# Sums of key weights moved behind row tile 5, and the steps of TensorE in a new order, in a two-branch linear-attention kernel

## The chip, the cores and the metric

The kernel runs on one core of a Trainium2 chip. The metric is the time of one execution on the device, in microseconds; the time before is the median of three runs. One further execution was taken with the hardware profiler, and all views of the profile are of that one. PE is TensorE's matmul, PEld its weight load, DVE is VectorE, ACT is ScalarE, POOL is GpSimd, SP is the engine that issues most DMAs. "L767" is line 767 of the kernel before.

## The reference

Two linear-attention blocks A and B share the input x (2048 x 640, bf16), each with its own weights; 32 heads of 20 columns. A sigmoid gate mixes them.

```python
def _A_ref(x, wqkv, wo):
    qkv = (x @ wqkv).reshape(B, S, 3, H, Dh).transpose(2, 0, 3, 1, 4)
    q, k, v = qkv[0], qkv[1], qkv[2]
    phi = lambda t: jnp.where(t > 0, t + 1, jnp.exp(t)) + 1e-6
    pq, pk = phi(q), phi(k)
    kv = jnp.einsum("bhsd,bhse->bhde", pk, v)
    z = jnp.einsum("bhsd->bhd", pk)
    num = jnp.einsum("bhqd,bhde->bhqe", pq, kv)
    den = jnp.einsum("bhqd,bhd->bhq", pq, z)[..., None] + 1e-6
    o = num / den
    return o.transpose(0, 2, 1, 3).reshape(B, S, D) @ wo
...
x = A_x
g = _sigmoid((x * gate_w).sum(-1, keepdims=True))
a = _A_ref(x, A_wqkv, A_wo)
b = _B_ref(x, B_wqkv, B_wo)
return g * a + (1 - g) * b
```

`_B_ref` is the same function with B's weights.

## The kernel before

Rows of x are worked in 16 tiles of 128. The program is made of operations (`Op`), each for one engine, with the buffers it reads and writes. A list scheduler inside the kernel (`Sched.run`) places them by estimated costs: on VectorE and ScalarE it takes the operation that can start soonest, ties by `prio`; on TensorE it keeps the order in which they were made. So TensorE's order is written out by hand, and the queues of VectorE, ScalarE, SP and GpSimd follow from it. Each queue then runs in order on the chip, with semaphore waits where an operation needs another engine's result. PSUM has 8 banks; a step that takes a bank waits until its last reader is done.

The stages, in TensorE's order:

- K, row tiles 0 to 9, in the order of the loop over `t` (`k_both`, L651 and L652): the keys of A, then of B, five pairs of matmuls each, into two banks. `k_post` makes phi of them: ScalarE's exponential (L699), VectorE's minimum and addition (L702), and then either ScalarE's relu (L711, L726) and a VectorE addition (L717 for both branches at once, L729 for one), or VectorE's L738, which reads the banks itself. `s_pair` (L887) makes differences of the results, which the next stage needs.
- The string `MAIN` orders all that follows. A token names a step:
  - `K14A`: the keys of row tile 14, branch A. `K6.n`: step n of `ks_unit` (L815), which makes the keys of row tiles 12 and 13 in both branches with 7 products in place of 8 (Strassen's scheme, in Winograd's form). It needs sums of the key weights of A and B (`kw_sums`, L767, four VectorE operations) and differences of x (`kx_sums`, L787). Its results are put together on VectorE (`kcm`).
  - `Gg.n`: unit g (0 to 4) of the product of phi(k) transposed with x, in steps 1 to 9 (L1164). VectorE's L1197 (`c11`, `c12`, `c22`) and ScalarE's L1192 and L1271 read the banks; results are moved by transposing DMAs on SP into GSA and GSB.
  - `Qg.n` (L1043): the queries of unit g, first half of the rows; `R0.n` the same for unit 0 of the second half, `R1A` and the like (L1132) the other units of the second half, ten matmuls into two banks, whose readers are ScalarE's L1143 and L1149 or VectorE.
  - `kvA`, `kvB` (L1312): key-value products, from GSA and GSB. `wA0` ... `wB1` (L1344): times the output weights. `dA0` ... `dB1` (L1418): denominators. `T1` stands for four VectorE sums of the resulting weights, `Sb` for VectorE's differences (L1519) of the queries of row block b, `X2` for sums of x, `LA` for a load.
  - `Oi.n` (L1554): the output of 256 rows, pair i (0 to 7), step n of 7. Steps 3 and 4 end with the stores of 128 rows each. ScalarE's L1593, L1570, L1598, L1619 and VectorE's L1577 read the banks.

The sums of key weights use the weights of both branches alone. They are made in the loop over row tiles, where the call stands:

```python
    for t in range(2, KT):
        k_both(t, "AB" if t in RELUB else "A")
        if t % 2:
            s_pair(t // 2)
        if t == 4:
            kw_sums()
    t_all(0, 8)
    kx_sums()
```

Though the call comes behind tile 4, nothing but their inputs holds the four operations back, and the scheduler put them as soon as VectorE had a place for them: among the operations of tiles 0 to 2.

Of the kernel before, what the change touches and what calls it, by code (L numbers as in the profile page):

```python
# [47 lines left out]
KT = 10  # L48
KU = 6
KJ = 7  # L50
KRS = ("10A", "10B", "11A", "11B", "12A", "13B", "14A", "14B", "15A", "15B", "8A", "9A", "9B",)
MAIN = """K14A K6.1 K10A K6.2 K6.5 K6.6 K14B K6.3 K10B K6.7 K11A K11B K6.4 K15A K15B G2.1 G1.1 G2.8 G0.1 G3.1
G1.8 G0.2 G0.8 G0.9 G1.2 G2.2 G2.9 G3.2 G0.6 G0.5 G1.9 G0.7 G3.8 G1.6 G0.3 G2.6 G1.5 G1.7 G0.4 G2.5
G1.3 Q1.1 G2.7 G1.4 Q1.2 Q1.5 Q1.6 G3.9 G3.6 G2.3 Q1.7 Q1.3 Q0.1 Q1.4 Q4.5 Q4.1 Q0.2 Q0.6 Q0.5 G2.4
Q4.6 Q4.2 Q0.7 kvA X2 Q0.3 G4.1 Q4.3 G4.2 G3.5 Q0.4 G4.8 Q4.7 G3.7 Q2.5 G3.3 Q2.1 G3.4 Q3.1 Q2.6
Q2.3 G4.5 Q2.7 G4.6 Q4.4 Q2.2 G4.7 Q3.6 Q3.5 Q3.2 Q3.7 Q2.4 G4.9 G4.3 Q3.4 G4.4 Q3.3 wA0 dA0 R1A
wA1 LA dB0 S1 S0 kvB R4A wB0 R2B R4B R1B wB1 T1 R3B R0.1 R3A R2A R0.6 R0.5 O1.1
R0.2 R0.7 O1.5 R0.3 O3.1 O0.1 O1.2 O3.2 R0.4 O0.2 O3.5 O1.6 O2.1 O1.3 O3.6 O0.6 O2.2 O2.5 O3.7 dA1
dB1 S2 S3 O2.6 O2.3 O1.7 O2.7 O3.3 O0.5 O2.4 O3.4 O0.7 O4.1 O5.1 O6.1 O1.4 O5.2 O4.2 O0.4 O6.2
O5.5 O4.5 O4.6 O7.5 O5.6 O6.6 O6.5 O5.3 O5.7 O6.7 O7.1 O4.7 O5.4 O4.3 O6.3 O7.6 O0.3 O4.4 O7.7 O6.4  # L60
O7.2 O7.3 O7.4"""
RS = (0,)
PB = {}
PQH = (0,)
# [45 lines left out]
class Sched:  # L110
# [9 lines left out]
    def op(self, eng, fn, cost, ins=(), outs=(), after=(), prio=None, name="", dma=None):  # L120
        if eng == "ACT" and dma is None:
            after = list(after) + self.consts
        o = Op(eng, fn, cost, list(ins), list(outs), after, (self.base or len(self.ops)) if prio is None else prio, name, dma)
        self.ops.append(o)
        return o
# [184 lines left out]
def body(nc, A_x, A_wqkv, A_wo, B_x, B_wqkv, B_wo, gate_w, out, log=None):  # L310
# [150 lines left out]
    def dve2(n):  # L461
        return 150 + 0.53 * n
# [178 lines left out]
    pk_last = []  # L641
# [104 lines left out]
    def k_both(t, relu):  # L746
        units = []
        for X in XS:
            ps = Buf("k", "ps", 2, cover=(512, 128))
            for c in range(NC):  # L750
                k_step(X, t, c, ps)
            units.append((X, ps, X in relu))
        k_post(t, units)
# [3 lines left out]
    def kw_sums():  # L757
        a1, a2, b1, b2 = [WK[X][:, c : c + 2, 0 : D + 1] for X in XS for c in (0, 2)]

        def kw(k):  # L760
            return KW[k][:, :, 0 : D + 1]

        for k, in0, in1, how, need in ((1, b1, a1, ALU.subtract, ()), (2, kw(1), b2, ALU.add, (1,)), (3, b1, b2, ALU.add, ()), (4, a2, kw(2), ALU.subtract, (2,))):
            bkw[k] = Buf("kw")
            op(
                "DVE",
                lambda e, k=k, in0=in0, in1=in1, how=how: e.tensor_tensor(out=kw(k), in0=in0, in1=in1, op=how),  # L767
                dve2(1282),
                ins=[bwk[X, c] for X in XS for c in range(4)] + [bgc, bwz] + [bkw[j] for j in need],
                outs=[bkw[k]],  # L770
                name="kw",
            )

# [26 lines left out]
    def ks_unit(j):  # L800
# [22 lines left out]
        def comb(ps, src, into_src):  # L823
            return op(
                "DVE",
                lambda e: e.tensor_tensor(out=kqg(src), in0=psx(ps), in1=kqg(src), op=ALU.add)
                if into_src
                else e.tensor_tensor(out=psw(ps, D + 1), in0=psw(ps, D + 1), in1=KQ[src.slot][:, 0 : D + 1], op=ALU.add),
                dve1(D + 1),
                ins=[ps, src],  # L830
                outs=[src if into_src else ps],
                name="kcm",
            )
# [3 lines left out]
        def step(n):  # L837
# [11 lines left out]
            elif n == 3:  # L849
                mm(pz, D + 1, False, [(WK["B"][:, 2 + c, :], KX[4][:, c, :]) for c in range(2)] + [(WK["B"][:, 4, :], KX[5])], [bkx[4], bkx[5], bgc] + [bwk["B", c] for c in range(2, 5)], [d[5]])  # L850
                comb(pz, s2, False)
                k_post(t1, [("A", py, "%dA" % t1 in KRS), ("B", pz, "%dB" % t1 in KRS)])
            elif n == 7:
                mm(px, D + 1, False, [(KW[3][:, c, :], KX[3][:, c, :]) for c in range(2)], [bkw[3], bkx[3]], [d[2]])
                d[7] = comb(px, s5, True)
            elif n == 4:
                mm(px, D, False, [(KW[4][:, c, :], xt(2 + c, 1)) for c in range(2)] + [(WK["A"][:, 4, :], xt(4, 1))], bx + [bkw[4], bwk["A", 4]], [d[7]])
                for X, ps in (("B", s5), ("A", px)):
                    k_post(t2, [(X, ps, "%d%s" % (t2, X) in KRS)])

# [5 lines left out]
    def s_pair(j):  # L866
        if j % 2 == 0:
            return
        r = range(j - 1, j + 1)
        pk = [bpk[X, t] for X in XS for t in range(2 * j - 2, 2 * j + 2)]  # L870
        for u0, u1 in ((0, 1), (1, NPU)) if j == 7 else ((0, NPU),):

            def pv(h, k):
                return PKv[:, 2 * u0 + h : 2 * u1 : 2, k, j - 1 : j + 1, :]

            def sv(k):
                return SSv[:, u0:u1, k, j - 1 : j + 1, :]

            def sub(out, a, b, ins, d, name):
                bb = Buf(name)  # L880
                for x in r:
                    for u in range(u0, u1):
                        d[u, x] = bb
                s_op.append(
                    op(
                        "DVE",
                        lambda e: e.tensor_tensor(out=out, in0=a, in1=b, op=ALU.subtract),  # L887
                        dve2(2 * (u1 - u0) * 128),
                        ins=ins,
                        outs=[bb],  # L890
                        name=name,
                    )
                )

            k = (u0, j)
            sub(sv(0), pv(1, 0), pv(1, 1), pk, bs1, "s1")
            sub(sv(1), pv(0, 0), sv(0), pk + [bs1[k]], bs2, "s2")
            sub(sv(2), pv(0, 1), sv(1), pk + [bs2[k]], bs4, "s4")
            sub(pv(1, 0), pv(1, 0), pv(0, 0), pk + [bs1[k]], bs3, "s3")
# [48 lines left out]
    for t in range(2, KT):  # L948
        k_both(t, "AB" if t in RELUB else "A")
        if t % 2:  # L950
            s_pair(t // 2)
        if t == 4:
            kw_sums()
    t_all(0, 8)
    kx_sums()
# [203 lines left out]
    def prod(g, name, ps, reg, mov, w, first, ins, after=(), js=(0, 8)):  # L1159
        for j0, j1 in ([(j, j + 1) for j in range(*js)] if g == 0 else [js]):  # L1160

            def fn(e, j0=j0, j1=j1):
                for j in range(j0, j1):
                    r = e.matmul(PS[:, ps.slot, 0:w], reg[:, j, :], mov(j, w), start=(first and j == 0), stop=(j == 7), skip_group_check=not first)  # L1164
                return r

            i = []
            for j in range(j0, j1):
                i += [b for b in ins(j) if b not in i]
            last[name] = op("PE", fn, (j1 - j0) * mm_cost(w), ins=i, outs=[ps], after=after, name="%s_%d" % (name, g))  # L1170
# [3 lines left out]
    def g_unit(g):  # L1174
# [10 lines left out]
        def xv(h, right):  # L1185
            return lambda j, w: (xr if right else xl)(h, j, j + 1, w)[:, 0, :]
# [58 lines left out]
        def step(n):  # L1245
            if n in (1, 8):
                prod(g, "P1", px, ra1, xv(0, False), W, True, lambda j: xn(j, 0) + [bpk[one[0], 2 * j]], js=(0, KJ) if n == 1 else (KJ, 8))
            if n in (2, 9):
                prod(g, "P2", py, ra2, xv(1, False), HC, True, lambda j: xn(j, 1) + [bpk[one[0], 2 * j + 1]], js=(0, KJ) if n == 2 else (KJ, 8))
            if n == 8:  # L1250
# [377 lines left out]
    qsteps = []  # L1628
    kleft = len([t for t in MAIN.split() if t[0] == "K"])
    ks, kps, ktiles, kdone = ks_unit(KU), {}, set(), {j for j in (1, 3, 5) if 2 * j + 1 < KT}  # L1630
    for tok in MAIN.split():
        sch.base = None if tok[0] == "K" else 10**5
        if tok[0] == "K":
# [4 lines left out]
            else:  # L1638
                X, t = tok[-1], int(tok[1:-1])
# [3 lines left out]
                if X == "B":  # L1643
                    k_post(t, [(Y, kps[Y, t], "%d%s" % (t, Y) in KRS) for Y in XS])
                    ktiles.add(t)
# [60 lines left out]
def bass_gated_mix__linear_attn_block__linear_attn_block__prompt_kernel(nc, *args):  # L1706
    body(nc, *args)
# [28 lines left out]
```

## Time and profile before

| | |
|---|---|
| time, median of 3 runs | 175.81 us (175.81 to 176.22) |
| time of the profiled execution | 175.72 us |
| its span in the trace | 174.3 us |
| granted TensorE clock | 1.00 |
| instructions | 3365 |

Where the span goes, by the costliest groups of TensorE and the group that the change moves (line, engine, operation, tiles, shape, count, busy us, mean ns, idle before):

```profile
L651 PE MATMUL ps<-WKW,XT 128*128 128x512 bf16 x140 | 39.4, 382 | 0.2
...
L1164 PE MATMUL ps<-TX,PKS 128*128 128x321 bf16 (+1 forms) x160 | 24.1, 300 | 0.0
L1164 PE MATMUL ps<-XN,PKS 128*128 128x321 bf16 (+1 forms) x120 | 18.3, 300 | 0.0
```

A matmul's busy time covers its whole way through the array, and the next one starts well before it ends: a pair of L651 and L652 comes every 0.27 us, though the two have 0.60 us of busy time. So gaps of TensorE are read from the starts, not from the busy time. Idle time of the other engines costs nothing as long as TensorE goes on.

### The profile page before, as it was taken

The page shows a single profiled execution, that of the slowest core. Times are in us where ns is not written, and L with a number is a line of the kernel's source. Part 1 is how long each engine was busy: PE and PEld are TensorE (multiplying, and loading weights), DVE is VectorE, ACT ScalarE, POOL GpSimd, SP SyncE. Part 2 cuts the span into 40 slices and gives each one's busy share as a digit, 9 for nine tenths or more (in the row PEclk, how much of TensorE's full clock was granted, in tenths as well). Part 3 has the DMA queues.
Part 4 walks back from the last instruction along what each step waited for, and adds up shares of the span by engine and source line. Part 5 has one row for each costly group of instructions (what it writes and reads, how often), then busy time and mean ns, then how long its engine had stood idle before and what let it go on. Part 6 is the DMA issues. An engine that isn't in the chain of part 4 may idle for free.

```text
span 174.3 us, 3365 instructions
## 1 busy us (share of the span) xinstructions
PE 171.6 (98%) x1331; PEld 107.7 (62%) x1331; DVE 140.1 (80%) x246; ACT 115.0 (66%) x221; POOL 4.9 (3%) x17
## 2 busy tenths in 40 slices
PE   9999999999999999999999999999999999999995
PEld 5455555555577776655766655655556667776773
DVE  2298996999999937678975798799999985989441
ACT  5378889998952323558594888848899874366133
POOL 2000000000000080000000000000000000000000
PEclk9999999999999999999999999999999999999999
DMA  6989999990000025310732703277670011451144
GB/s 196 286 152 202 172 367 365 358 171 8 4 0 0 0 41 98 75 38 0 156 79 56 211 0 75 53 196 199 224 184 26 0 41 30 94 186 41 38 148 153
DMA packets 33035, 20.59 MB, mean 118 GB/s; under 512 B 18260, under 2 KB 32892, under 8 KB 33020
## 3 DMA queue, kind: packets, MB, share of 16 engines
q1 hardware_dynamic: 32062, 19.76, 43.4%
q10 hardware_dynamic: 958, 0.63, 1.2%
q8 instruction: 10, 0.16, 0.4%
q14 instruction: 5, 0.04, 0.1%
HBM read 10.88 MB, written 4.26 MB: 87 GB/s over the span
## 4 chain that ended last, share of the span: by engine, by line
PE 96%; DMA 2%; SPq 0%; ACT 0%; issue 0%
PE ps L1164 22%; PE ps L1554 22%; PE ps L651 17%; PE ps L1043 13%; PE ps L1132 10%; PE ps L652 4%; PE ps L815 3%; DMA WKW<-in_A_wqkv_dram 2%; PE ps L1418 1%; PE ps L1344 1%; PE ps L1312 1%; SPq L444 0%; ACT PKS L1619 0%; PE ps L628 0%
## 5 line engine op out<-in xcount | busy, mean ns | idle before, releaser
L651 PE MATMUL ps<-WKW,XT 128*128 128x512 bf16 x140 | 39.4, 382 | 0.2
L652 PE MATMUL ps<-WKW,XT 128*128 128x128 bf16 (+1 forms) x140 | 30.9, 220 | 0.0
L699 ACT ACTIVATE EKT<-ps 128x640 bf16<-128x640 f32 x31 | 21.5, 709 | 5.3 <-PE ps L652 4.8
L651 PEld LDWEIGHTS ps<-WKW,XT 128*128 128x128 bf16 x140 | 13.8, 99 | 17.2 <-DMA WKW<-in_A_wqkv_dram 0.5
L1164 PE MATMUL ps<-TX,PKS 128*128 128x321 bf16 (+1 forms) x160 | 24.1, 300 | 0.0
L1164 PEld LDWEIGHTS ps<-TX,PKS 128*128 128x128 bf16 x160 | 15.6, 98 | 7.4
L1164 PE MATMUL ps<-XN,PKS 128*128 128x321 bf16 (+1 forms) x120 | 18.3, 300 | 0.0
L1164 PEld LDWEIGHTS ps<-XN,PKS 128*128 128x128 bf16 x120 | 11.7, 98 | 5.4
L1192 ACT ACTIVATE EKT<-ps 128x321 f32<-128x321 f32 (+1 forms) x15 | 6.5, 438 | 12.7 <-PE ps L1164 9.0
L652 PEld LDWEIGHTS ps<-WKW,XT 128*128 128x128 bf16 x140 | 13.8, 98 | 0.0
L887 DVE TENSOR_TENSOR PKS<-PKS 128x1280 bf16<-128x1280 bf16 (+2 forms) x20 | 13.1, 684 | 0.1
L1073 ACT ACTIVATE EQ<-ps 128x512 bf16<-128x512 f32 x18 | 10.6, 600 | 3.8 <-DVE ps L1057 2.4
L711 ACT ACTIVATE PKS<-ps 128x640 bf16<-128x640 f32 x16 | 11.3, 708 | 0.0
L1143 ACT ACTIVATE EQ<-ps 128x1024 bf16<-128x1024 f32 x8 | 8.2, 1029 | 4.4 <-PE ps L1132 3.5
L702 DVE TENSOR_SCALAR EKT<-EKT 128x1280 bf16<-128x1280 bf16 (+1 forms) x19 | 8.2, 437 | 3.6 <-ACT EKT L699 3.5
L1043 PE MATMUL ps<-XT,WQA 128*128 128x512 bf16 x36 | 10.4, 379 | 0.0
L1197 DVE TENSOR_TENSOR WKW<-ps,EKT 128x320 bf16<-128x320 f32 x15 | 7.3, 485 | 2.8 <-PE ps L1164 2.6
L1132 PE MATMUL ps<-XT,WQA 128*128 128x512 bf16 x40 | 9.2, 381 | 0.0
L1132 PE MATMUL ps<-XT,WQB 128*128 128x512 bf16 x40 | 9.0, 381 | 0.0
L1619 ACT ACTIVATE PKS<-ps 128x320 bf16<-128x320 f32 x8 | 3.5, 437 | 8.1 <-PE ps L1554 8.1
L738 DVE SCALAR_TENSOR_TENSOR PKS<-ps,EKT 128x640 bf16<-128x640 f32 x10 | 8.1, 818 | 0.0
L1577 DVE TENSOR_TENSOR PKS<-ps,EKT 128x320 bf16<-128x320 f32 x9 | 4.4, 492 | 4.1 <-PE ps L1554 3.8
(179 smaller groups left out, 324.6 us busy)
## 6 DMA issues: line engine op xcount, KB each, us to landing
out_dram<-PKS SPq DMA_DIRECT2D x15, 160.0 KB, 1.8
XN<-in_A_x_dram SPq DMA_DIRECT2D x1, 2240.0 KB, 9.3
WKW<-in_A_wqkv_dram SPq DMA_DIRECT2D x5, 160.0 KB, 3.9
WKW<-in_B_wqkv_dram SPq DMA_DIRECT2D x5, 160.0 KB, 4.3
WQA<-in_A_wqkv_dram SPq DMA_DIRECT2D x1, 800.0 KB, 10.9
WQB<-in_B_wqkv_dram SPq DMA_DIRECT2D x1, 800.0 KB, 12.2
WVA<-in_A_wqkv_dram SPq DMA_DIRECT2D x1, 800.0 KB, 12.0
PKS<-in_B_wqkv_dram SPq DMA_DIRECT2D x1, 800.0 KB, 4.9
```

The source lines that it names most:

```text
L651: e.matmul(a[:, 0:512], l, WK[X][:, c, 0:512], start=(c == 0), stop=(c == NC - 1))
L652: return e.matmul(a[:, 512:w], l, WK[X][:, c, 512:w], start=(c == 0), stop=(c == NC - 1))
L699: op("ACT", lambda e, i=i, ps=ps: e.activation(evg(i), psg(ps), ACT.Exp), act_cost(D), ins=[ps] + first, outs=[ek, b], name="ke")
L702: lambda e: e.tensor_scalar(EK[:, ek.slot : ek.slot + n, :], EK[:, ek.slot : ek.slot + n, :], 1.0, EPS, op0=ALU.min, op1=ALU.add),
L711: op("ACT", lambda e, X=X, ps=ps: e.activation(pkt(X, t), psg(ps), ACT.Relu), act_cost(D), ins=[ps], outs=[rk], name="kr")
L887: lambda e: e.tensor_tensor(out=out, in0=a, in1=b, op=ALU.subtract),
L1043: r = e.matmul(PS[:, ps.slot, :], w, x, start=(first and i == 0), stop=(i == len(prs) - 1), skip_group_check=not first)
L1073: o = [op("ACT", lambda e: e.activation(EQ[:, eq.slot + h, :], pv(), ACT.Exp), act_cost(512), ins=ins, outs=[eq], name="qe")]
L1132: r = e.matmul(PS[:, ps.slot + h, :], WQ[X][:, c, g::5], XT[:, c, 1024 + 512 * h : 1536 + 512 * h], start=(c == 0), stop=(c == NC - 1))
L1143: op("ACT", lambda e: e.activation(ev(), pv(), ACT.Exp), act_cost(1024), ins=[ps], outs=[eq], name="qe"),
L1164: r = e.matmul(PS[:, ps.slot, 0:w], reg[:, j, :], mov(j, w), start=(first and j == 0), stop=(j == 7), skip_group_check=not first)
L1554: r = e.matmul(PS[:, ps.slot, 0:HALF], reg(g), mov(g), start=(first and g == 0), stop=(g == NC - 1), skip_group_check=not first)
```

## The change

Two edits. `kw_sums` is called behind row tile 5 instead of 4, and its operations now have to wait for the last phi operation made so far, that of row tile 5 (L717). And `MAIN` is a new order of the same steps: each token of the old string stands once in the new one, at another place in most cases.

```diff
+KWT = 5
-MAIN = """K14A K6.1 K10A K6.2 K6.5 K6.6 K14B K6.3 K10B K6.7 K11A K11B K6.4 K15A K15B G2.1 G1.1 G2.8 G0.1 G3.1
-G1.8 G0.2 G0.8 G0.9 G1.2 G2.2 G2.9 G3.2 G0.6 G0.5 G1.9 G0.7 G3.8 G1.6 G0.3 G2.6 G1.5 G1.7 G0.4 G2.5
-G1.3 Q1.1 G2.7 G1.4 Q1.2 Q1.5 Q1.6 G3.9 G3.6 G2.3 Q1.7 Q1.3 Q0.1 Q1.4 Q4.5 Q4.1 Q0.2 Q0.6 Q0.5 G2.4
-Q4.6 Q4.2 Q0.7 kvA X2 Q0.3 G4.1 Q4.3 G4.2 G3.5 Q0.4 G4.8 Q4.7 G3.7 Q2.5 G3.3 Q2.1 G3.4 Q3.1 Q2.6
-Q2.3 G4.5 Q2.7 G4.6 Q4.4 Q2.2 G4.7 Q3.6 Q3.5 Q3.2 Q3.7 Q2.4 G4.9 G4.3 Q3.4 G4.4 Q3.3 wA0 dA0 R1A
-wA1 LA dB0 S1 S0 kvB R4A wB0 R2B R4B R1B wB1 T1 R3B R0.1 R3A R2A R0.6 R0.5 O1.1
-R0.2 R0.7 O1.5 R0.3 O3.1 O0.1 O1.2 O3.2 R0.4 O0.2 O3.5 O1.6 O2.1 O1.3 O3.6 O0.6 O2.2 O2.5 O3.7 dA1
-dB1 S2 S3 O2.6 O2.3 O1.7 O2.7 O3.3 O0.5 O2.4 O3.4 O0.7 O4.1 O5.1 O6.1 O1.4 O5.2 O4.2 O0.4 O6.2
-O5.5 O4.5 O4.6 O7.5 O5.6 O6.6 O6.5 O5.3 O5.7 O6.7 O7.1 O4.7 O5.4 O4.3 O6.3 O7.6 O0.3 O4.4 O7.7 O6.4
-O7.2 O7.3 O7.4"""
+MAIN = """K6.1 K14A K6.5 K6.2 K6.6 K14B K6.3 K6.7 K10A K10B K6.4 K11A K11B K15A K15B G3.1 G3.8 G1.1 G2.1 G0.1
+G3.2 G2.8 G1.8 G1.2 G1.9 G3.9 G0.2 G0.8 G0.9 G2.2 G0.5 G0.6 G1.5 G0.3 G0.7 G1.6 G3.6 G0.4 G2.9 G2.6
+G2.5 Q4.1 G1.7 G1.3 G3.5 G2.7 G1.4 Q4.6 Q4.5 G2.3 Q4.2 Q4.7 G3.3 Q4.3 G2.4 Q1.1 Q0.1 kvA X2 Q1.6
+Q0.5 G3.7 Q0.2 Q0.6 Q4.4 Q1.5 Q0.7 Q1.2 G4.1 Q0.3 G4.8 Q1.7 G3.4 Q3.1 Q2.1 Q1.3 G4.2 Q3.6 Q1.4 G4.6
+Q3.2 Q2.5 Q2.6 Q2.2 G4.9 Q0.4 Q3.5 Q2.3 G4.5 Q3.7 Q2.7 G4.7 Q2.4 Q3.4 G4.3 G4.4 Q3.3 wA0 dA0 R4B
+wA1 LA dB0 S1 S0 kvB R4A wB0 R1A R2B R2A wB1 T1 R3A R0.1 R1B R3B R0.6 R0.5 O2.1
+O3.5 R0.7 R0.2 O1.1 R0.3 O0.1 O2.2 O1.2 R0.4 O0.2 O3.1 O2.6 O1.6 O3.2 O0.5 O3.6 O3.3 O1.5 O1.7 dA1
+dB1 S3 S2 O1.3 O2.5 O3.7 O2.7 O2.3 O3.4 O1.4 O2.4 O0.6 O0.3 O4.1 O7.1 O6.1 O0.7 O4.2 O5.1 O6.2
+O7.2 O5.2 O4.5 O4.6 O5.5 O6.5 O5.6 O4.7 O6.6 O0.4 O6.3 O6.7 O4.3 O7.6 O7.5 O5.7 O5.3 O7.7 O7.3 O4.4
+O5.4 O6.4 O7.4"""
...
                 outs=[bkw[k]],
+                after=pk_last[-1:],
                 name="kw",
...
-        if t == 4:
+        if t == KWT:
             kw_sums()
```

All other lists that steer the kernel (which engine does which copy, which tiles use relu, priorities) stay as they were. In the built program the four sums now stand in VectorE's queue behind L717 of tile 5, with L702 of tile 6 between the third and the fourth. In SP's queue the move of GSB's second part and the load of B's value weights come sooner among their neighbours, and the stores of the output stand in another order.

## The prediction

> **What bounds the kernel now.** I read the page first: share of each engine, then the chain that ended last. After that came the timelines of TensorE, VectorE and ScalarE around the places that the diff moves.
>
> ```profile
> PE 171.6 (98%) x1331; PEld 107.7 (62%) x1331; DVE 140.1 (80%) x246; ACT 115.0 (66%) x221; POOL 4.9 (3%) x17
> ...
> PE 96%; DMA 2%; SPq 0%; ACT 0%; issue 0%
> ```
>
> TensorE is busy nearly all the time and makes up 96% of the chain. So the time is the sum of its matmuls plus the gaps between them, and an edit elsewhere counts only where it opens or closes such a gap. I went through the starts of all 1331 matmuls for gaps that are not the stream itself. Past the first 5 us (loads of the first weights) there is one wait, of 0.28 us. The rest are the turns into, within and out of six short blocks, `kvA`, `wA0 dA0`, `wA1 dB0 kvB`, `wB0`, `wB1`, `dA1 dB1`, near 0.1 us each. The wait in TensorE's timeline:
>
> ```profile
> 12.29 0.38 PE L651 MATMUL ps<-WKW,XT 128*128 128x512 bf16 x1
> 12.51 0.22 PE L652 MATMUL ps<-WKW,XT 128*128 128x129 bf16 x1
> 12.84 0.38 PE L651 MATMUL ps<-WKW,XT 128*128 128x512 bf16 x1
> ```
>
> A pair L651, L652 takes 0.27 us (12.02, 12.29), so the pair at 12.84 was due at 12.56. It is the first of row tile 3, A. Its two PSUM banks are those of tile 0, B, which VectorE's L738 has to read first. VectorE then:
>
> ```profile
> 10.59 0.83 DVE L767 TENSOR_TENSOR GSA<-GSA,WKW 128x1282 bf16<-128x1282 bf16 x1
> 11.32 0.63 DVE L702 TENSOR_SCALAR EKT<-EKT 128x640 bf16<-128x640 bf16 x2
> 11.88 1.55 DVE L738 SCALAR_TENSOR_TENSOR PKS<-ps,EKT 128x640 bf16<-128x640 f32 x2
> 13.34 0.82 DVE L767 TENSOR_TENSOR GSB<-WKW 128x1282 bf16<-128x1282 bf16 x1
> 14.07 0.49 DVE L702 TENSOR_SCALAR EKT<-EKT 128x1280 bf16<-128x1280 bf16 x1
> ```
>
> L767 are the sums of key weights. Two of the four ran before 11.4, and pushed the first L738 of the pair at 11.88 to an end at 12.69; TensorE went on at 12.84.
>
> **The change part by part.**
>
> *Sums out of tiles 0 to 2.* Without them, L702 of tile 0, B starts when ScalarE's exponential ends (10.04 + 0.70 = 10.74) and L738 follows: 10.8 + 0.33 + 0.04 + 0.82 = 12.0, before 12.56. The gap closes: -0.28. Nothing else was late there: the transposed x of tile 3 landed at 10.5.
>
> *Sums behind tile 5.* Four at the spacing seen in VectorE's rows (0.73 from start to start; a little more where one reads another) are 2.95 us of VectorE. They now wait for L717 of tile 5, which ends near 24.2. Behind them in VectorE's queue stand the L702, L729, L738 of tile 6, then tile 7. What can take them up is VectorE's idle time right there, 0.35 + 1.42 = 1.77 us:
>
> ```profile
> 24.86 0.49 DVE L702 TENSOR_SCALAR EKT<-EKT 128x1280 bf16<-128x1280 bf16 x1 [0.35 <-ACT EKT L699]
> ...
> 28.04 0.49 DVE L702 TENSOR_SCALAR EKT<-EKT 128x1280 bf16<-128x1280 bf16 x1 [1.42 <-ACT EKT L699]
> ```
>
> The rest is carried on, as VectorE is full afterwards:
>
> ```profile
> 24.00:36.00 12.00, 12.00 (x91) 6.81 (x90) 10.11 (x20) 10.79 (x21) 0.00 (x0) 1.00 1.07 349
> 36.00:48.00 12.00, 12.00 (x91) 6.84 (x90) 11.83 (x16) 11.20 (x24) 0.00 (x0) 1.00 0.25 48
> 48.00:56.00 8.00, 8.00 (x61) 5.73 (x60) 7.65 (x16) 3.26 (x8) 0.00 (x0) 1.00 0.00 0
> ```
>
> (columns: PE, PEld, DVE, ACT, POOL busy). I laid the changed order of VectorE by hand on these durations, with TensorE 0.28 earlier. Tile 6 B leaves its banks at 28.8; the step that now takes them, K6.1, comes at 31.6. The sums are ready by 27.7, first used by K6.5 at 33.5. The two additions L815's units need end near 38.9 and 40.1, for K6.4 at 41.15. Tile 10 is done at 45.2 for G3.1 at 47.4, tile 11 at 50.5 for G3.2 at 51.4, tile 15 at 52.4 for G1.9 at 53.6. The first L1197 ends at 54.5, and G2.2, which takes its bank, comes at 55.06. So the smallest margin is 0.55 us, and I take this part at 0. With the cover gone it costs what lateness exceeds that margin: 0 to 2.0 us (worked out under the first rival). ScalarE's exponentials of tiles 8 and 9 wait for buffers that VectorE frees at 24.2 and 28.8, and start at 27.8 and 30.4: not later than now.
>
> The row above shows the VectorE op after a sum starting at 14.07, 0.09 before that sum ends (13.34 + 0.82). [...]
>
> *New order of TensorE.* Same 372 steps, same matmuls, same six blocks: nothing by itself. What counts is which step now comes sooner after the work that it waits for. Two shrink clearly.
>
> First, kvA after G2.3. Between them lay 13 steps (7.5 us), now 7 (4.6 us). G2.3 ends, VectorE adds, SP issues the transposing move of GSA, and it lands:
>
> ```profile
> L1312 PE MATMUL ps<-GSA,WVA x55: 186/194/217, 82.6 to 83.5; 128*64 128x60 bf16 x50, 128*64 128x40 bf16 x5
> ...
> L444 SPq DMA_TRANSPOSE GSA<-WKW x5: 1199/1200/1222, 62.4 to 75.7; - x5
> ...
> DMA to landing us min/median/max: 2.6/2.6/3.1
> ```
>
> The last issue stands at 75.7, 0.6 after G2.3's last matmul; 0.6 + 2.6 to 3.1 is 3.2 to 3.7 of the 4.6 us. SP has nothing else queued there (the move before is issued 2 us sooner). Taken at 0; if the move waited a whole issue (1.2 us) in SP, +0.3.
>
> Second, the last steps of the R stretch. ScalarE's queue there is full, and ends with the L1143 that frees the two banks of the last whole-width R step:
>
> ```profile
> 123.67 1.03 ACT L1149 ACTIVATE XT<-ps 128x1024 bf16<-128x1024 f32 x1
> 123.94 1.55 ACTq L444 DMA_DIRECT2D wpsB<-TX  x2
> ...
> 131.77 1.06 ACT L1143 ACTIVATE EQ<-ps 128x1024 bf16<-128x1024 f32 x1
> ```
>
> ```profile
> 132.72 0.81 PE L1043 MATMUL ps<-PKS,WQB 128*128 128x512 bf16 x3
> 133.37 0.84 PE L1554 MATMUL ps<-PKS,PQ 128*128 128x320 bf16 x5
> ```
>
> It ends at 132.83; the step that takes the banks (O3.1) starts at 133.37, with 0.54 to spare. In the new order the step in that place, O1.1, comes before R0.3 (0.65 us: 132.72 to 133.37), not behind it, while ScalarE has the same nine instructions and its two DMA issues to do. Both 0.28 earlier: banks free at 132.55, O1.1 due at 132.44. That is -0.11; the smallest margin without a gap in this trace is 0.06 (O4.6 at 157.74, its operand at 157.69). So a new gap of some 0.15 us. Bounds: 0, if ScalarE saves the pause of 0.11 before its op at 127.58; 0.35, if the chain is 0.2 later.
>
> Other waits with short margins keep at least 0.2 us by the same hand-work (Q1.6 behind kvA, O0.2, and O2.6 behind T2). The end of the program keeps its last step, O7.4, and the last store; four full stores now come 0.68 apart before it, each 0.33 of SP's time: 0, bound +0.2.
>
> **Sum.** -0.28 + 0.15 = -0.13 us on a span of 174.3, so 174.2, and the profiled execution's 175.72 becomes 175.6. The median of the runs shown is 175.81, 0.09 above it: 175.7.
>
> **The rivals.**
>
> *VectorE falls behind at the change from K to G (slower).* Against the old schedule, 0.28 earlier, the first L1197 starts at 53.3; to end before 55.0 it may start 1.2 us later. By hand it is 0.7 later. If the idle 1.77 us are not won back (the exponentials slip with the buffers), VectorE is 2.95 + 0.28 = 3.2 late, and TensorE waits 2.0; with the idle time used, but the 1.2 us left over plus 0.28 carried in full, 0.3. Middle 1.1: 175.81 - 0.28 + 1.1 = 176.6. It decides from a lateness of 1.2 us at that L1197 on. For it: VectorE busy 11.83 of 12. Against: the waits up to it all have 0.8 us or more.
>
> *All gaps closed.* O1.1 does not wait: 175.81 - 0.28 = 175.5. For it: the bound 0 above. More cannot be had: after 5 us there is no other wait to remove.
>
> *The first gap stays* (the change does not do what it says): another release of the same banks is late by as much, and O1.1 adds 0.15: 176.0. Against: L702's only other input is ScalarE's 10.74.
>
> **How the numbers follow.** Forecast 0.45, all gaps closed 0.20, first gap stays 0.06, VectorE behind by enough to cost over 0.8 us 0.20, another late wait of over 0.7 us among the many moved steps 0.05, something that wins over 0.5 us 0.04. I call 0.3% (0.53 us) what a measurement of this kernel can tell from no change. The first three lie inside it: 0.71; slower 0.25; faster 0.04. The predicted time is the forecast's, 175.7. Its own range is 175.5 to 175.9. The wide one goes from 175.35 (dense, and runs 0.15 below) up into the first rival, 176.6.
>
> **What would show it.** Right: L651 of tile 3 follows 0.06 us behind its predecessor; four L767 rows (one line lower) between 24 and 28; VectorE without its idle 1.42 near 28; G2.2 without a gap near 55; a gap of 0.1 to 0.2 near 132.4 ended by ScalarE. Wrong: gaps of TensorE between 33 and 56 ended by VectorE, a wait of kvA near 80 on the move of GSA, or a span below 173.9.

## The result and the profile after

| | before | changed |
|---|---|---|
| median, 22 runs each | 175.98 us (175.58 to 176.75) | 175.51 us (175.04 to 176.0) |
| ratio | | 0.9975, 95% interval 0.9964 to 0.9986 |
| span of the profiled execution | 174.3 us | 173.8 us |
| time of the profiled execution | 175.72 us | 175.2 us |

The changed kernel was measured twice more beside the experiments below: 0.9994 (0.9981 to 1.0007, 12 runs) and 0.9990 (0.9975 to 1.0005, 12 runs). Weighted by the number of runs that is (22 x 0.9975 + 12 x 0.9994 + 12 x 0.9990) / 46 = 0.9984, or 0.28 us of 175.98. Worked out from the single times of the three measurements, the 95% interval of that is about 0.1 to 0.4 us.

In the changed kernel lines from 652 to 740 are one higher than before, those past 772 two. First the page after: shares of the engines, and the chain that ended last, by engine.

```profile
PE 171.3 (99%) x1331; PEld 107.6 (62%) x1331; DVE 140.1 (81%) x246; ACT 115.3 (66%) x221; POOL 5.3 (3%) x17
...
PE 99%; ACT 0%; issue 0%; DVE 0%
```

TensorE's share of the chain went from 96% to 99%. That is not the wait, which was 0.2% of the span: the chain before began with the load of the first weights (3.95 us, 2.3%), and the chain of this profile does not. The wait at row tile 3 in TensorE's timeline after (start, duration, engine, line, tiles):

```profile
12.06 0.38 PE L652 MATMUL ps<-WKW,XT 128*128 128x512 bf16 x1
12.27 0.22 PE L653 MATMUL ps<-WKW,XT 128*128 128x129 bf16 x1
12.33 0.38 PE L652 MATMUL ps<-WKW,XT 128*128 128x512 bf16 x1
```

Pairs stand 0.27 apart, across the place where 0.28 us of waiting stood. The four sums in VectorE's timeline after:

```profile
23.18 0.82 DVE L718 TENSOR_TENSOR PKS<-PKS,EKT 128x1280 bf16<-128x1280 bf16 x1
24.11 0.83 DVE L768 TENSOR_TENSOR GSA<-WKW 128x1282 bf16<-128x1282 bf16 x1
24.85 0.83 DVE L768 TENSOR_TENSOR GSB<-WKW 128x1282 bf16<-128x1282 bf16 x1
25.59 0.83 DVE L768 TENSOR_TENSOR GSA<-GSA,WKW 128x1282 bf16<-128x1282 bf16 x1
26.33 0.49 DVE L703 TENSOR_SCALAR EKT<-EKT 128x1280 bf16<-128x1280 bf16 x1
26.73 0.83 DVE L768 TENSOR_TENSOR GSB<-WKW,GSA 128x1282 bf16<-128x1282 bf16 x1
27.47 0.48 DVE L730 TENSOR_TENSOR PKS<-PKS,EKT 128x640 bf16<-128x640 bf16 x1
```

They begin 0.11 behind the L718 that they wait for, the first three 0.74 from start to start, and VectorE's idle 1.42 us near 28 is gone. The table by stage after (columns: window, its length, busy us of PE, PEld, DVE, ACT, POOL, then granted clock, DMA share, GB/s):

```profile
24.00:36.00 12.00, 12.00 (x90) 6.80 (x89) 11.89 (x23) 10.88 (x21) 0.00 (x0) 1.00 1.07 345
36.00:48.00 12.00, 12.00 (x91) 6.93 (x90) 11.91 (x18) 11.56 (x25) 0.00 (x0) 1.00 0.20 41
48.00:56.00 8.00, 8.00 (x61) 5.75 (x59) 7.75 (x13) 2.73 (x6) 0.00 (x0) 1.00 0.00 0
```

VectorE is now full from 24 to 53.6 us (11.89 where it was 10.11), yet TensorE has no wait there. The starts of all matmuls show no wait past 5 us in this profile, only the turns of the six blocks, near 0.1 us each as before.

The two spans differ by 0.5, not 0.28. The other 0.24 lies in the first 7 us, where both kernels do the same (the first matmul of row tile 0, B at 6.88, before at 7.12). This is scatter: the three profiles of the changed kernel differ among themselves by as much as 0.9 us in their first 6.3 us, so one profile can't tell a change of a few tenths, and the gaps inside it have to.

### The profile page after: what moved, and what is told of

Its sections match the earlier page's. It is cut to its first block, busy times and chain, and to the rows that moved or that the text cites. A ratio compares the mean times of both kernels' runs of the same rounds, so it can differ in the third digit from the quotient of the medians.

```text
span 173.8 us, 3365 instructions
## 1 busy us (share of the span) xinstructions
PE 171.3 (99%) x1331; PEld 107.6 (62%) x1331; DVE 140.1 (81%) x246; ACT 115.3 (66%) x221; POOL 5.3 (3%) x17
## 4 chain that ended last, share of the span: by engine, by line
PE 99%; ACT 0%; issue 0%; DVE 0%
PE ps L1166 22%; PE ps L1556 22%; PE ps L652 18%; PE ps L1045 13%; PE ps L1134 10%; PE ps L653 5%; PE ps L817 3%; PE ps L579 1%; PE ps L1420 1%; PE ps L1346 1%; PE ps L1314 1%; PE ps L592 1%; ACT PKS L1621 0%; DVE ONE L477 0%; PE ps L629 0%
## 5 line engine op out<-in xcount | busy, mean ns | idle before, releaser
L652 PE MATMUL ps<-WKW,XT 128*128 128x512 bf16 x140 | 38.9, 381 | 0.0
L712 ACT ACTIVATE PKS<-ps 128x640 bf16<-128x640 f32 x16 | 11.4, 722 | 0.0
L703 DVE TENSOR_SCALAR EKT<-EKT 128x1280 bf16<-128x1280 bf16 (+1 forms) x19 | 8.2, 435 | 3.7 <-ACT EKT L700 3.6
L1145 ACT ACTIVATE EQ<-ps 128x1024 bf16<-128x1024 f32 x8 | 8.2, 1028 | 4.3 <-PE ps L1134 3.6
L1579 DVE TENSOR_TENSOR PKS<-ps,PKS 128x320 bf16<-128x320 f32 x11 | 5.4, 490 | 5.2 <-PE ps L1556 4.9
L1199 DVE TENSOR_TENSOR WKW<-ps,EKT 128x320 bf16<-128x320 f32 x15 | 7.2, 486 | 2.8 <-PE ps L1166 2.6
L1572 ACT ACTIVATE PKS<-ps 128x320 f32<-128x320 f32 x11 | 4.8, 441 | 5.9 <-PE ps L1556 5.9
L739 DVE SCALAR_TENSOR_TENSOR PKS<-ps,EKT 128x640 bf16<-128x640 f32 x10 | 8.2, 820 | 0.1
```

The lines of the kernel that those rows point to most:

```text
L652: e.matmul(a[:, 0:512], l, WK[X][:, c, 0:512], start=(c == 0), stop=(c == NC - 1))
L703: lambda e: e.tensor_scalar(EK[:, ek.slot : ek.slot + n, :], EK[:, ek.slot : ek.slot + n, :], 1.0, EPS, op0=ALU.min, op1=ALU.add),
L712: op("ACT", lambda e, X=X, ps=ps: e.activation(pkt(X, t), psg(ps), ACT.Relu), act_cost(D), ins=[ps], outs=[rk], name="kr")
L739: lambda e, X=X, i=i, ps=ps: e.scalar_tensor_tensor(pkt(X, t), psg(ps), 0.0, evg(i), op0=ALU.max, op1=ALU.add),
```

## The experiments

All edits are against the changed kernel. "Before" is the kernel before on the same chip.

### The sums alone

```diff
-MAIN = """K6.1 K14A K6.5 K6.2 K6.6 K14B K6.3 K6.7 K10A K10B K6.4 K11A K11B K15A K15B G3.1 G3.8 G1.1 G2.1 G0.1
...
+MAIN = """K14A K6.1 K10A K6.2 K6.5 K6.6 K14B K6.3 K10B K6.7 K11A K11B K6.4 K15A K15B G2.1 G1.1 G2.8 G0.1 G3.1
...
```

> The sums behind tile 5, the order of before. Theory A (the gain is the 0.28 us gap of TensorE at tile 3, the new order only hides the later sums): the first matmul of tile 3 follows its predecessor by 0.06 us, -0.28; VectorE is some 0.7 us later than before from K6 on, in an order not laid out for it, so new gaps of 0.1 to 0.8 us in all between 40 and 58 us of the span: between -0.2 and +0.5 against before. Theory B (the order makes the gain): within 0.1 of before.

Measured: 181.3 us, ratio 1.0303 (1.0268 to 1.0337), 5.5 us over the kernel before. The six executions fall into two groups: three of 180.46 to 180.57 us, and three of 182.03 to 182.28, the profiled one among them. The wait at tile 3 is gone, and much more is lost elsewhere. TensorE's timeline:

```profile
44.53 0.22 PE L653 MATMUL ps<-WKW,XT 128*128 128x129 bf16 x1
46.74 0.72 PE L817 MATMUL ps<-GSB,XT 128*128 128x512 bf16 x4 [2.00 <-DVE PQ L828]
47.30 0.43 PE L817 MATMUL ps<-WKW,XT 128*128 128x512 bf16 x2
47.57 0.57 PE L652 MATMUL ps<-WKW,XT 128*128 128x512 bf16 x1
47.93 0.31 PE L653 MATMUL ps<-WKW,XT 128*128 128x128 bf16 x1
48.04 0.63 PE L652 MATMUL ps<-WKW,XT 128*128 128x512 bf16 x1
```

K6.4 (L817) waits for VectorE's L828. In VectorE's queue L828 now stands behind an L730 and an L739 (43.99 and 44.40; L828 at 45.86); in the kernel before the same operation (L826, 42.87) came ahead of them (44.74 and 45.14). So it is the order of VectorE's queue that makes this wait, and not only its load. Matched against the profile of before matmul by matmul (both have the same order), the 6.6 us between the two spans are: start +0.39, tile 3 -0.26, a wait at 42.8 us +0.31, K6.4 +2.17, half clock behind it (granted 0.50 from 48 to 50 us) +1.69, and four waits past 107 us of 0.48, 0.87, 0.51 and 0.41. New waits were expected, but for -0.2 to +0.5 us against before in all; the size was missed, and a loss in the second half, far from the sums, was not expected at all.

### The order alone

```diff
-KWT = 5
+KWT = 4
...
-                after=pk_last[-1:],
```

> The new order, the sums called behind tile 4 and free to run early, as before. Theory A: the gap of 0.28 us at tile 3 is back, ended by VectorE's L738; the rest dense; the time is that of before within 0.15 us, and 0.25 to 0.45 over the changed kernel. Theory B: 0.3 to 0.45 us under before, like the changed kernel.

Measured: 176.47 us, 1.0039 (1.0022 to 1.0056). The wait at tile 3 is back (pairs 12.84 and 13.18: 0.28 too late), and there is a new one of 0.31 at K6.4 (41.69 to 42.06), behind the same operation of VectorE, and two of 0.06, one of them ahead of O1.1. Theory A had the place but not the size: it gave a time within 0.15 us of before, and 0.68 over it was measured. So the order makes no gain by itself, and the two edits belong together: either one alone is slower than the kernel before.

### O1.1 one step sooner

```diff
-O3.5 R0.7 R0.2 O1.1 R0.3 O0.1 O2.2 O1.2 R0.4 O0.2 O3.1 O2.6 O1.6 O3.2 O0.5 O3.6 O3.3 O1.5 O1.7 dA1
+O3.5 R0.7 O1.1 R0.2 R0.3 O0.1 O2.2 O1.2 R0.4 O0.2 O3.1 O2.6 O1.6 O3.2 O0.5 O3.6 O3.3 O1.5 O1.7 dA1
```

> The changed kernel with O1.1 one step sooner (in front of R0.2, 0.65 us). The prediction had a gap before O1.1, of 0.15 us; the trace of the changed kernel shows its banks freed by ScalarE at 132.04 and O1.1 at 132.21. Theory A (that wait was rightly named, only the lateness of ScalarE's chain mis-sized): O1.1 due at 131.56, so a gap of 0.5 to 0.65 us, and the kernel 0.5 us over the changed one, at before's time or 0.1 over. Rival (O1.1 does not hang on that chain): no gap, the changed kernel's time.

Measured: 176.69 us, 1.0050 (1.0033 to 1.0066). O1.1 started at 132.08 without a wait; the scheduler had put ScalarE's queue in another order, and a later step waited 0.77 for L1078, which now stood behind. Neither expectation was met. The run says nothing of the wait that it was made for, only that one step's exchange makes two new waits of 0.77 and 0.21 us through the queues laid around it, and a time 0.9 us over the kernel before.

### The sums on GpSimd, early

```diff
-                "DVE",
+                "POOL",
...
-                dve2(1282),
+                2600.0,
...
-                after=pk_last[-1:],
```

> The changed kernel with the four sums on GpSimd, not held back, so that VectorE has 3 us less to do before 48 us. Theory A (TensorE is dense after 5 us, VectorE's load costs nothing any more): the changed kernel's time within 0.1 us. Rival (VectorE's fullness between 24 and 48 us still costs something): another 0.1 to 0.4 us faster. If the sums are late on GpSimd, a gap at K6.5 near 33 us, ended by GpSimd.

Measured: 179.17 us, 1.0213 (1.0176 to 1.0250). Both expectations missed. The first sum in GpSimd's timeline of this run, and VectorE beside it:

```profile
8.60 2.61 POOL L768 TENSOR_TENSOR GSA<-WKW 128x1282 bf16<-128x1282 bf16 x1 [7.31 <-DMA WKW<-in_B_wqkv_dram]
```

```profile
8.78 2.61 DVE L703 TENSOR_SCALAR EKT<-EKT 128x640 bf16<-128x640 bf16 x1
11.43 0.82 DVE L739 SCALAR_TENSOR_TENSOR PKS<-ps,EKT 128x640 bf16<-128x640 f32 x1
```

TensorE's timeline behind it:

```profile
12.31 0.39 PE L652 MATMUL ps<-WKW,XT 128*128 128x512 bf16 x1 [0.98 <-DVE PKS L739]
```

L703 takes 0.33 us elsewhere for 640 columns and 0.49 for 1280. Beside the four GpSimd operations it takes 2.61, 1.87, 1.88 and, with 1280 columns, 2.09, and ends 0.2 to 0.3 behind each; L739, one of whose inputs is in PSUM, keeps 0.82 (11.43, beside the second). TensorE pays 1.15, 1.37 and 0.48 us for it, and waits for another 0.8 us in three places later on.

### Which part of the order

The new order among the first 15 tokens alone, K6.1 to K15B:

```diff
-K6.1 K14A K6.5 K6.2 K6.6 K14B K6.3 K6.7 K10A K10B K6.4 K11A K11B K15A K15B G3.1 G3.8 G1.1 G2.1 G0.1
...
+K6.1 K14A K6.5 K6.2 K6.6 K14B K6.3 K6.7 K10A K10B K6.4 K11A K11B K15A K15B G2.1 G1.1 G2.8 G0.1 G3.1
...
```

> The changed kernel with the new order only among the first 15 tokens (K6.1 to K15B), and the order of before from G2.1 on; sums behind tile 5. Theory A (the new order matters where VectorE is behind, which is the K part: in the run with all of the old order the whole loss began at K6.4, 2.16 us of wait): no wait above 0.5 us at K6.4, time 175.4 to 176.6. Rival B (the turn to the G steps matters as well: the order of before begins with G2.1, the new one with G3.1, and VectorE is still some us behind there): a wait of 0.5 us or more between 45 and 60 us, time 176.7 to 179. Rival C (the order in the second half carries the gain): waits past 100 us as with all of the old order, 0.5 to 1.5 us, time 176 to 177.3.

Measured: 177.9 us, 1.0124 (1.0107 to 1.0141). K6.4 does not wait, and there is no wait between 45 and 60 us: the K part is what hides the sums from TensorE, and rival B falls. All that is lost lies past 107 us. TensorE's timeline (in this run's kernel the lines past 772 are one higher than before, not two):

```profile
108.73 2.11 PE L1133 MATMUL ps<-XT,WQA 128*128 128x512 bf16 x9 [0.66 <-ACT GSA L1362]
...
116.72 6.67 PE L1133 MATMUL ps<-XT,WQB 128*128 128x512 bf16 x29 [0.81 <-DVE PKS L1148]
...
133.71 0.63 PE L1044 MATMUL ps<-WVA,GSA 128*128 128x512 bf16 x2 [0.35 <-ACT PKS L1053]
...
139.24 0.85 PE L1555 MATMUL ps<-PKS 128*128 128x320 bf16 x5 [0.21 <-ACT ps L1594]
```

Against the kernel before they are worth 0.48, 0.87, 0.51 and 0.41, the same four as with the sums alone. Rival C has the place, at more than its size. But TensorE's order there is that of before, which had no such waits. What differs is the order of the operations on ScalarE and VectorE: the scheduler, with the estimates shifted by the new K part, laid some eighteen of them past 107 us otherwise. The next run has TensorE's old second half with the old queues.

### The new order in the first half alone

The new order up to Q3.3, the old one from wA0 on:

```diff
-Q3.2 Q2.5 Q2.6 Q2.2 G4.9 Q0.4 Q3.5 Q2.3 G4.5 Q3.7 Q2.7 G4.7 Q2.4 Q3.4 G4.3 G4.4 Q3.3 wA0 dA0 R4B
...
+Q3.2 Q2.5 Q2.6 Q2.2 G4.9 Q0.4 Q3.5 Q2.3 G4.5 Q3.7 Q2.7 G4.7 Q2.4 Q3.4 G4.3 G4.4 Q3.3 wA0 dA0 R1A
...
```

> The changed kernel with the new order up to Q3.3 (block branch A, the first 97 tokens) and the order of before from wA0 on; sums behind tile 5. With this the queues of ScalarE and VectorE past 107 us are the same, operation by operation, as in the kernel before, which they were not in the run with the new order among the first 15 tokens alone. Theory (the 2.3 us of waits past 107 us of that run came from how the planner laid the other engines' queues there, not from the old order of TensorE's second half as such): no wait past 107 us beyond what the kernel before has, time 175.4 to 176.0. Rival (the second half of the order has to be new once the sums have moved): waits at about 108, 116, 133 and 139 us as there, time 177.3 to 178.2.

Measured: 175.67 us, 0.9982 (0.9971 to 0.9994). No wait past 107 us beyond those of before. So the second half did not have to be new, and the waits of the two runs above came from the queues laid beside it. This version is as fast as the changed kernel, not measurably faster.

### How much more VectorE can take

One more sum, then four more, written to a free place:

```diff
-                lambda e, k=k, in0=in0, in1=in1, how=how: e.tensor_tensor(out=kw(k), in0=in0, in1=in1, op=how),
+                lambda e, k=k, in0=in0, in1=in1, how=how: [e.tensor_tensor(out=w, in0=in0, in1=in1, op=how) for w in ([TXf[:, 1296 * i : 1296 * i + 1282].rearrange("p (c f) -> p c f", c=2) for i in range(1)] if k == 4 else []) + [kw(k)]][-1],
```

(`range(4)` in the second.)

> The changed kernel with a fifth sum of the same size on VectorE (0.74 us from start to start), written to a free place and read by nothing. Theory (the sums hide because VectorE's lag is smaller than its margins: 1.03 us at K6.4, 0.88 at G2.3, 0.46 and an idle 0.25 ahead of it at G2.2): 0.74 stays under all of these but the last, which it passes by 0.03: time as the changed kernel's on this chip, within 0.2 us. Rival (the cover is thinner than single margins say, since a late VectorE also gives banks back later): 0.3 to 0.8 us slower, with a wait between 40 and 57 us.

Measured: 175.64 us, 0.9988 (0.9975 to 1.0001), beside 175.80 for the changed kernel. One wait of 0.10 us, at 46.25, for ScalarE's L712. The theory holds: all but 0.10 of the 0.74 us is hidden. The place is new: neither this expectation nor the prediction had ScalarE's L712 among the margins, and in the changed kernel it ends at 45.55, only 0.25 before TensorE goes on in its banks at 45.80.

> The changed kernel with four more sums of the same size on VectorE (2.96 us), written to a free place and read by nothing. Theory A (each us past the margin is one us of TensorE): first wait at K6.4 near 41 us, 2.96 - 1.03 = 1.9 us, the rest of the lag (0.3) at G2.2; together 2.25 us, TensorE at full speed afterwards: 177.5 to 178.1 if the changed kernel stands at 175.5. Rival B (a wait of about 2 us also halves TensorE's clock for some 4 us, as seen behind the wait in the run with the sums alone moved): the same wait, then pairs of matmuls of 512 columns every 0.53 us instead of 0.27 for about 4 us; VectorE catches up in that time and the wait at G2.2 is gone: 179 to 180.5.

Measured: 177.96 us, 1.0125 (1.0109 to 1.0141): 2.16 us over the changed kernel, where theory A had 2.25. The sum came out right, the places did not. TensorE's first waits:

```profile
32.18 0.72 PE L817 MATMUL ps<-WKW,XT 128*128 128x512 bf16 x4 [0.17 <-DVE PKS L739]
...
33.51 0.39 PE L652 MATMUL ps<-WKW,XT 128*128 128x512 bf16 x1 [0.61 <-ACT GE L691]
```

K6.1 waits first, for the banks of tile 6 B that L739 gives back late; then come waits of 0.2 to 0.8 us up to 48.6, each for work of another engine that itself waited for VectorE. TensorE's mean granted clock is 1.00 in all four executions.

### The changed kernel again, twice

No edit. The first run:

> The changed kernel once more, as the mark for the three runs beside it and for the start, whose times differ from one profile to the next (the first matmul of row tile 2 at 9.61 to 10.25 us in the profiles so far). If the change is worth the one gap at row tile 3 (0.28 us) and the rest of its first result (0.44) was scatter of the start: 0.2 to 0.4 us under the kernel before. If it is worth more than the gap: 0.4 to 0.7 us under.

Measured: 175.80 us, 0.9994 (0.9981 to 1.0007), 0.11 us under before by the ratio, less than either expectation. Its span is 175.0, 1.2 more than the first profile's: 0.92 in the first 6.3 us, 0.08 in between, and 0.19 ahead of O1.1. ScalarE's rows, then TensorE's:

```profile
124.38 1.83 ACTq L445 DMA_DIRECT2D wpsB<-TX  x2
126.26 1.02 ACT L1145 ACTIVATE EQ<-ps 128x1024 bf16<-128x1024 f32 x1 [1.15 <-DVE PKS L1487]
...
132.26 1.08 ACT L1145 ACTIVATE EQ<-ps 128x1024 bf16<-128x1024 f32 x1
```

```profile
132.56 0.81 PE L1045 MATMUL ps<-XT,WQA 128*128 128x512 bf16 x3
133.40 0.85 PE L1556 MATMUL ps<-PKS,PQ 128*128 128x320 bf16 x5
```

The last L1145 ends at 133.34, O1.1 (L1556) was due 0.65 behind 132.56, at 133.21, and starts at 133.40. The same place in the first profile:

```profile
123.46 1.23 ACTq L445 DMA_DIRECT2D wpsB<-TX  x2
124.73 1.02 ACT L1145 ACTIVATE EQ<-ps 128x1024 bf16<-128x1024 f32 x1 [0.55 <-issue]
...
130.99 1.06 ACT L1145 ACTIVATE EQ<-ps 128x1024 bf16<-128x1024 f32 x1
```

There the two DMA issues (L445) held ScalarE 1.23 us and not 1.83, the chain ended at 132.05, and O1.1 followed at 132.21, in its turn.

The second run:

> The changed kernel a third time, beside the other two. The two ratios so far are 0.9975 and 0.9994, with 22 and 12 runs. If the wait at row tile 3 (0.28 us) is all that the change is worth, less some 0.1 for O1.1 where ScalarE's issues are slow: 0.1 to 0.35 us under the kernel before. If the first result was the truer: 0.35 to 0.6 under.

Measured: 175.92 us, 0.9990 (0.9975 to 1.0005), 0.05 under before by the medians and 0.18 by the ratio, which lies in the first expectation; the interval, up to 0.44 under, reaches into the second as well. The issues took 1.36 us and O1.1 did not wait. The whole drift against the first profile, 0.80 us, lies in the first 6.3 us.

### The issues off ScalarE's queue

```diff
-                    "ACT" if X == "B" and r == 0 else "SP",
+                    "SP",
```

> The changed kernel with the four transfers of the output-weight products that ScalarE's queue issued (two at about 124 us, 0.87 to 1.83 us of its time in the profiles so far) issued by SyncE's queue instead. Theory (whether TensorE waits ahead of O1.1 is settled by how long these two issues hold ScalarE: 1.23 us gave no wait, 1.83 gave 0.19): ScalarE's chain to O1.1 is free of them, O1.1 has a margin of 0.5 us or more in every profile, and the time is 0 to 0.2 us under the changed kernel beside it. Rival (SyncE's queue, now with five issues in a row, brings the products late to the first step that reads them): a wait of 0.3 to 1 us past 130 us, time 0.2 to 0.9 above. A second rival (ScalarE waits at 126 us for VectorE anyway, so its chain starts no sooner): the margin at O1.1 is as before, time the same.

Measured: 175.87 us, 0.9990 (0.9978 to 1.0001), beside 175.92. The last L1145 ends at 132.53 and O1.1 starts at 132.93: a margin of 0.40, not 0.5, since ScalarE's operations ahead of that L1145 now wait for TensorE's steps (0.22 and 0.16 us). No step waits for the later moves. In this profile it takes the chance of the 0.19 away; a measurement of the time can't tell it.

### One long wait

The profile with the sums alone had shown half clock behind a wait of 2 us, that with four more sums none behind several short ones. Here 3.3 us of VectorE work stand right ahead of the operation that K6.4 waits for:

```diff
-                lambda e: e.tensor_tensor(out=kqg(src), in0=psx(ps), in1=kqg(src), op=ALU.add)
+                lambda e: [e.tensor_tensor(out=w, in0=XT[:, 0, 0:n], in1=XT[:, 1, 0:n], op=ALU.add) for w, n in [(TXf[:, 5248 + 1312 * i : 6528 + 1312 * i], 1280) for i in range(4)] + [(GSBf[:, 2592:3200], 608)]] and e.tensor_tensor(out=kqg(src), in0=psx(ps), in1=kqg(src), op=ALU.add)
```

> The changed kernel with 3.3 us of more work on VectorE (four sums of 1280 columns and one of 608, read by nothing) right ahead of the operation that K6.4 waits for, so that its margin of 1.03 us becomes one wait of about 2.3 us, where four more sums behind tile 5 made several waits of 0.2 to 0.8. Theory (the half clock of 4 us behind K6.4 in the run with the sums alone moved came from the wait of 2.0 us itself): pairs of matmuls every 0.53 us instead of 0.27 for 3 to 5 us behind the wait, 4.0 to 5.0 us over the changed kernel: 179.5 to 180.8. Rival (it takes a longer wait, and something else slowed that run): pairs every 0.27 us straight after the wait, a further 0.3 us at G2.2 at most, 2.3 to 2.7 us over: 177.9 to 178.5.

Measured: 178.4 us, 1.0127 (1.0099 to 1.0155). TensorE's timeline:

```profile
44.40 0.72 PE L817 MATMUL ps<-GSB,XT 128*128 128x512 bf16 x4 [2.19 <-DVE PQ L828]
44.95 0.43 PE L817 MATMUL ps<-WKW,XT 128*128 128x512 bf16 x2
45.22 0.38 PE L652 MATMUL ps<-WKW,XT 128*128 128x512 bf16 x1
...
45.49 0.38 PE L652 MATMUL ps<-WKW,XT 128*128 128x512 bf16 x1
```

The wait is longer than the one that was followed by half clock, and pairs go on every 0.27 us, at a granted clock of 1.00 from 44 to 52 us. The rival holds: a wait of this length does not by itself halve the clock.

## Why the prediction was right, point by point

- *TensorE is dense, one wait to gain, -0.28.* Held: the wait is gone in every profile of a kernel with the sums behind tile 5, and back at 0.28 with the sums early. Over 46 runs the change is worth 0.28 us; that this agrees to the last digit is chance, since the three measurements gave 0.11 to 0.44 (by their ratios) and the interval is 0.1 to 0.4. The time alone could not tell 0.28 from the 0.13 of the forecast; the gap in the traces does.
- *Sums behind tile 5 cost nothing.* Held for the two edits together. Of VectorE's own margins the hand-laid order had the thinnest nearly right: the first L1199 ended at 54.33 and G2.2 took its bank at 54.79, a margin of 0.46 where 0.55 was said; ahead of that L1199 VectorE idled 0.25. But the smallest margin of the stretch was not there: ScalarE's L712 left 0.25 at 45.80, and one more sum made TensorE wait there, for 0.10, and not at G2.2. Four more cost 2.16. The sums that do not read one another again started 0.09 before the one ahead ended (24.85, against 24.11 + 0.83).
- *New order costs nothing by itself; kvA in time.* kvA started at 79.73 without a wait. The last transposing move that it reads was issued at 75.6 and moves of this kind land after 2.6 to 3.1 us: the allowance of 4.6 was enough.
- *A new gap of 0.15 ahead of O1.1.* This term was mis-sized for the first profile: 0 there. The mechanism was right and its bounds (0 to 0.35) held. The prediction took ScalarE's chain as moved 0.28 sooner with its two issues at 1.55 us; in the first profile they took 1.23 and the chain began 0.8 sooner, in the second 1.83 and the gap was 0.19. Over seven profiles with this order of TensorE the issues took 0.81 to 1.83 us: 1.83 made TensorE wait 0.19, the two of 1.58 made it wait 0.06 (the order alone) and 0.02 (four more sums), and 1.36 or less not at all. So even at the 1.55 us that the prediction assumed, some 0.05 would have been nearer than 0.15. A term that hangs on a duration with such scatter is a chance, not an amount.
- *The rivals.* "All gaps closed" (175.5) is what the first profile shows. That the first median, 175.51, hits its number is luck: the same kernel gave 175.80 and 175.92 later, and the forecast's 175.7 lies between them. "VectorE behind" did not come, and its price was right as far as tried: past some 0.7 us of more work TensorE loses nearly one us for each (2.96 us more cost 2.16). "The first gap stays" fell.
- *What the prediction did not see:* how much hung on the two edits being made together. The sums alone lose 6.6 us in the profiled execution: 2.17 by the place of L828 in VectorE's queue, 1.69 by the clock, which only half of the executions pay, 2.3 by queues that the scheduler laid otherwise 60 us later. It compared only the two whole kernels, so this did not touch its sum.

## What to carry to other kernels

Where a scheduler derives the other queues from one written order, an edit in one place can cost in a far one: compare the order of every queue behind the edit, and take back what you don't need, as the old second half here. To learn how much cover a hidden piece of work has, add more of it bit by bit: the first wait names the thinnest place, which need not be on the engine that does the work, and the point from which the time rises is the margin. And for a change of a few tenths read the gap itself; the span and even the median of 20 runs scatter by more.

## What the runs showed of the hardware

- *The start scatters by when TensorE's pairs come twice as fast.* Rows of TensorE in the first profile of the changed kernel, then in its third:

```profile
4.37 0.38 PE L652 MATMUL ps<-WKW,XT 128*128 128x512 bf16 x1
...
4.67 0.39 PE L652 MATMUL ps<-WKW,XT 128*128 128x512 bf16 x1
```

```profile
4.26 0.63 PE L652 MATMUL ps<-WKW,XT 128*128 128x512 bf16 x1
...
4.81 0.61 PE L652 MATMUL ps<-WKW,XT 128*128 128x512 bf16 x1
...
5.32 0.63 PE L652 MATMUL ps<-WKW,XT 128*128 128x512 bf16 x1
...
5.86 0.55 PE L652 MATMUL ps<-WKW,XT 128*128 128x512 bf16 x1
```

Pairs go from 0.53 to 0.27 us apart at 4.3 us in the one, at 6.2 in the other; at 4.5 in the profile before, at 5.9 in the changed kernel's second, and before 3.8 with the new order in the first half alone, though TensorE is busy from 0.3 us on in all five. The granted clock reads 1.00 from 2 to 6 us in the first and the third alike, so it does not tell the two rates apart; what sets the moment was not shown. The first weights add to it: in the second profile a pair waited for their DMA and started at 5.34, 0.59 behind its turn (4.22 + 0.53).

- *Half clock behind a wait of 2 us, in half of the executions.* The table by stage of the run with the sums alone (the last but two columns: granted clock):

```profile
46.00:48.00 2.00, 1.26 (x8) 0.64 (x9) 2.00 (x3) 1.43 (x4) 0.00 (x0) 0.91 0.00 0
48.00:50.00 2.00, 2.00 (x9) 0.97 (x8) 2.00 (x5) 0.76 (x2) 0.00 (x0) 0.50 0.00 0
50.00:52.00 2.00, 2.00 (x13) 1.07 (x12) 1.56 (x3) 1.30 (x2) 0.00 (x0) 0.74 0.04 8
```

By the 0.91 and the 0.74 the clock fell at 47.64 and rose at 51.04, 3.40 us later; the pairs between stand 0.53 apart. Three of the six executions have a mean granted clock of 0.99 (182.03 to 182.28 us) and three of 1.00 (180.46 to 180.57): the same program pays for this in some executions and not in others, by about the 1.69 us found above. In the run with one long wait K6.4 waited 2.19 us, longer than the 2.00 here, and all four executions have a clock of 1.00. In the profile with the sums on GpSimd two waits of 0.98 and 1.20 us end at 12.31 and 15.05, and the clock stayed at 1.00 (one of that run's other five executions, the one of 181.37 us, has 0.99). So the length of a wait alone does not tell whether half clock follows it; what decides was not shown.

- *GpSimd and VectorE:* beside a GpSimd operation of 2.61 us a VectorE operation that takes 0.33 elsewhere took 2.61 and ended 0.18 behind it (above), so idle GpSimd was no free place for such work beside L703.
